# A third expert that runs on into the last ranking, one-hot products in place of a gather, and an order list made anew

## The chip, the cores and the metric

The kernel runs on one core of a Trainium2 chip. The metric is device microseconds of one execution, lower is better, given as the median of the runs shown. One more execution was taken with the hardware profiler, and all rows below are from it. Engines are named as in the profile: PE (TensorE matmul; PEld its weight loads), DVE (VectorE), ACT (ScalarE), POOL (GpSimd), SP (SyncE, which here issues DMAs only).

## The reference, cut to what matters

Two stages follow each other. The first is attention with a hash mask over 4 batches, 8 heads, 768 positions and 64 dimensions a head: a query sees a key only if all 6 sign bits of their projections agree. The second is a capacity expert: of each batch's 768 tokens the 128 with the highest gate score pass through a two-layer network and are added back.

```python
mask = q_bucket[:, :, :, None] == k_bucket[:, :, None, :]
scores = np.where(mask, scale * np.matmul(q, k.transpose(0, 1, 3, 2)), -1e9)
attn = np.exp(scores - np.max(scores, axis=-1, keepdims=True))
x = matmul(attn / (sum(attn) + 1e-9), v)      # then to (4, 768, 512)
scores = np.einsum('bsd,d->bs', x, w_gate)
for b in range(B):
    top_idx = np.argpartition(-scores[b], capacity)[:capacity]
    xe = x[b, top_idx]
    ye = np.maximum(xe @ w1, 0.0) @ w2
    out[b, top_idx] = xe + 1 / (1 + np.exp(-scores[b, top_idx]))[:, None] * ye
```

## The kernel before

There are 32 heads, numbered through all batches, so batch b is heads 8b to 8b+7. A head goes through these steps, each a small function that a word of a long list calls: load (X), split into two f16 parts (xh on ACT, xl on DVE), place by DMA (pa, pb, ps on SP's queue), row maxima in three pieces (mx and ma on PE, re on ACT, rd on DVE, line 550), scores in six units (s on PE, lines 584 and 587; e the exponential on ACT), a rest R = P minus its bf16 part in three pieces (two by r on DVE, line 617, one by g on POOL, line 620), the products with V in six chunks (a, line 642), the reciprocal (rc) and the normalised rows in the tile x (nw).

Three slots of two PSUM banks (`two`) and one of one bank (`one`) are shared by nearly all PE results; the string BANKS says which slot each use takes, and a use waits until the last reader of that slot is done.

The order in which each engine gets its instructions is written out by hand or by a planner in the string ORDER. A word is a function and its arguments, or the next step of a generator: c0 to c2 are `choose` (ranking of a batch), c3 `rank_last`, e0 to e2 `apply_expert`, e3 `apply_expert_last`. Every engine works its own instructions strictly in that order.

`turn` and `mine` deal with a resource that DVE and POOL share: an instruction of DVE with operands in SBUF is recorded by `mine`, and the next POOL subtraction (`turn`) waits for the last one recorded. Nothing makes the DVE instructions that come later wait for POOL.

For batches 0 to 2 `choose` makes the gate scores (line 694, tile `jks`, six instructions of 128x512, in two steps of three), turns them and sends them through DRAM, compares all pairs (lines 736 and 742), counts, makes a one-hot matrix `sel` (line 754), takes token numbers from it by products (line 803), and gathers the 128 chosen rows from `out` in DRAM by an indirect DMA. The expert then turns these rows (line 834), multiplies by w1 in three split products (line 870), takes the positive part, multiplies by w2 (line 892) and scatters the sum back (line 908).

For the last batch nothing follows that could cover this, so `rank_last` and `apply_expert_last` stand on the path to the end: scores, six f32 products that spread them over partitions (line 990), the comparisons, `sel`, the index product (line 1025), the index (line 1029), the gather, four transposes (line 834), the split (lines 842 to 846), and the two layers.

Of the kernel before, what the change touches and what calls it, by code (L numbers as in the profile page):

```python
# [52 lines left out]
ps.2.0 ma.1.0 rd.1.1 w vh.1 pb.1.2 rd.1.0 s.0.4 e.0.0 mt.1 vl.1 e.0.1 s.0.5 pb.1.3 mc2.1 mr.1 s.0.3 e.0.4 kv.2 X.7
pa.3.1 e.0.5 s.0.2 e.0.3 ps.3.0 mx.2.0 e.0.2 mx.2.2 sv.1 re.2.2 sh.1 r.0.0 re.2.0 a.0.0 r.0.2 mx.2.1 g.0.1 ma.2.2
sl.1 rd.2.2 a.0.1 ma.2.0 rd.2.0 re.2.1 xh.5 xh.7 s.1.3 ma.2.1 pa.4.0 s.1.0 s.1.2 rd.2.1 ps.3.1 pb.2.3 kv.3 pb.2.2
pb.3.2 e.1.3 pb.3.1 pb.3.3 e.1.0 X.8 pb.2.0 pb.2.1 xh.6 w a.0.2 xl.4 s.1.4 xl.5 xl.7 mt.2 mc2.2 mx.3.1 e.1.2 a.0.3
mr.2 pb.3.0 X.9 s.1.1 re.3.1 a.0.4 xl.6 mx.3.2 ma.3.1 e.1.1 a.0.5 rd.3.1 re.3.2 s.1.5 ma.3.2 h.1.0.4 e.1.4 rc.0
e.1.5 rd.3.2 pa.4.1 pb.4.0 g.1.1 nw.0 pa.5.0 sg.1.0.4 mx.3.0 r.1.0 re.3.0 s.2.0 ss.1.0.4 s.2.4 w s.2.1 ps.4.1
r.1.2 ma.3.0 e.2.0 e.2.4 s.2.2 a.1.0 s.2.3 e.2.1 e.2.2 a.1.1 rd.3.0 mt.3 w e.2.3 s.2.5 kv.4 mc2.3 ps.4.0 mx.4.0
pb.4.1 mx.4.2 pa.5.1 e.2.5 a.1.2 a.1.3 mr.3 g.2.1 re.4.0 mx.4.1 ma.4.0 r.2.0 ps.5.0 a.1.4 V.2 a.1.5 X.10 re.4.2  # L60
re.4.1 ma.4.2 s.3.5 w rd.4.0 ma.4.1 ps.5.1 xh.8 s.3.4 pb.4.2 w rd.4.2 pb.5.0 pa.6.0 rd.4.1 pa.6.1 pb.5.3 w e.3.5
e.3.4 s.3.0 mt.4 s.3.3 s.3.2 e.3.0 kv.5 mx.5.2 rc.1 nw.1 X.11 a.2.0 pb.4.3 mc2.4 e.3.3 mx.5.0 s.3.1 pb.5.2 re.5.2
# [124 lines left out]
def body(ctx, tc, qk, v, pj, wg, w1, w2, cst, cst16, out):  # L187
# [11 lines left out]
    def bank(name=None):  # L199
        return slots[int(next(banks))][:, 0]  # L200
# [521 lines left out]
    def put_out(b, half):  # L722
        d = slice(half * 256, half * 256 + 256)
        nc.scalar.dma_start(
            out[b].rearrange("(t p) d -> p t d", p=P)[:, :, d], st["x", b][:, :, d]
        )
# [369 lines left out]
```

## Time and profile before

| what | value |
|---|---|
| median of 3 runs | 421.06 us (420.73, 421.06, 422.6) |
| the profiled execution: its time | 423.3 us |
| its span, first to last instruction | 421.3 us |
| PE busy | 388.3 us, 92% of the span |
| DVE, ACT, POOL busy | 356.1, 287.2, 138.7 us |
| mean granted clock of TensorE | 0.969 of full |

The profiled execution lies 2.2 us above the median, and 2.0 us of it lie outside the span. Busy shares are means over the whole span, and this program has a long part in which PE hardly rests and a short part at its end in which it rests often, so they must be read by stretch.

### The profile page before, as it was taken

Reading aid. Unit: us, or ns where it says so; the run is one execution under the profiler, and the core shown is the slowest. Engines: PE = TensorE matmul, PEld = TensorE weight load, DVE = VectorE, ACT = ScalarE, POOL = GpSimd, SP = SyncE. Lnnn points to the kernel's source line nnn. Section 1 sums busy time; section 2 is a strip of 40 time slices with the busy share of each in tenths; the row PEclk is TensorE's granted clock in tenths of the full one; section 3 lists DMA queues with packets and bytes.
Section 4 is the critical chain, followed back from the end, with each engine's and each line's share of the span. In section 5 each row is a group of like instructions: output and inputs, shape, how many; then the busy total and the mean of one; then the engine's idle time right before and its main releaser. Section 6 shows DMA issues by size and latency. Waiting matters only on the chain.

```text
span 421.3 us, 13640 instructions
## 1 busy us (share of the span) xinstructions
PE 388.3 (92%) x5729; PEld 277.0 (66%) x5734; DVE 356.1 (85%) x585; ACT 287.2 (68%) x433; POOL 138.7 (33%) x91
## 2 busy tenths in 40 slices
PE   3799999999999999999799999999899999997385
PEld 1456776777667677786457777876557577875284
DVE  6879889899999999879979999769989898869521
ACT  4699988888889788866468787765667777441010
POOL 8115635243514284242432041250320434203000
PEclk9999999999999999999989999999989999999768
DMA  7746565383846542455445442325533331000500
GB/s 214 214 141 170 190 185 155 98 255 101 283 124 169 156 135 78 127 163 174 136 138 142 146 102 70 85 66 168 169 114 97 107 87 50 21 3 25 168 10 25
DMA packets 32940, 53.32 MB, mean 127 GB/s; under 512 B 5226, under 2 KB 24176, under 8 KB 32880
## 3 DMA queue, kind: packets, MB, share of 16 engines
q1 hardware_dynamic: 21696, 32.92, 27.9%
q10 hardware_dynamic: 10544, 17.43, 13.7%
q0 software_dynamic: 640, 2.10, 1.6%
q8 instruction: 45, 0.74, 0.8%
q14 instruction: 15, 0.12, 0.1%
HBM read 25.79 MB, written 7.35 MB: 79 GB/s over the span
## 4 chain that ended last, share of the span: by engine, by line
PE 70%; DVE 13%; issue 7%; DMA 5%; ACT 3%; SPq 1%; POOLq 0%; ACTq 0%; DVEq 0%
PE av L642 20%; PE two L584 11%; PE two L587 10%; PE two L524 6%; PE two L540 6%; PE one L870 3%; PE two L892 3%; PE one L584 3%; PE one L587 3%; DVE R L617 3%; DVE m L550 2%; PE two L331 2%; DMA A<-XH 2%; DVE jks L694 2%; DVE cm L736 1%
## 5 line engine op out<-in xcount | busy, mean ns | idle before, releaser
L620 POOL TENSOR_TENSOR R<-P 128x1536 f16<-128x1536 f32 x32 | 93.7, 2928 | 154.3 <-ACT P L600 25.3
L642 PEld LDWEIGHTS <-P 128*128 128x128 bf16 x2304 | 118.5, 97 | 17.4 <-issue 0.7
L642 PE MATMUL av<-V,P 128*128 128x65 f16 (+1 forms) x2304 | 123.6, 193 | 0.0
L642 PE MATMUL av<-V,R 128*128 128x65 f16 x1152 | 119.0, 192 | 0.0
L617 DVE TENSOR_TENSOR R<-P 128x1536 f16<-128x1536 f32 x64 | 114.8, 1804 | 2.7 <-ACT P L604 2.5
L604 ACT ACTIVATE P<-two 128x1024 f32<-128x1024 f32 x96 | 96.6, 1020 | 29.2 <-PE two L587 28.9
L550 DVE TENSOR_REDUCE m<-two 128x2 fp32r<-128x770 f32 x96 | 89.5, 952 | 20.4 <-PE two L540 20.1
L642 PEld LDWEIGHTS <-R 128*128 128x128 f16 x1152 | 105.5, 98 | 0.0
L584 PE MATMUL two<-A 97*128 97x512 f16 (+1 forms) x266 | 92.9, 357 | 5.9 <-DVE m L550 5.1
L587 PE MATMUL two<-B 128*128 128x512 f16 (+1 forms) x266 | 92.8, 356 | 0.0
L531 ACT ACTIVATE two<-two 128x770 f32<-128x770 f32 x96 | 75.0, 795 | 18.3 <-PE two L524 17.8
L587 PEld LDWEIGHTS <-B 128*128 128x128 f16 x384 | 38.1, 99 | 29.0 <-issue 7.8
L584 PEld LDWEIGHTS <-A 97*128 97x128 f16 x384 | 38.1, 99 | 25.9 <-issue 2.7
L524 PE MATMUL two<-kd,A 96*128 96x385 f16 x192 | 45.4, 330 | 3.5 <-DMA A<-sg 2.4
L540 PE MATMUL two<-A 96*128 96x385 f16 x192 | 46.4, 329 | 0.5 <-ACT two L531 0.5
L600 ACT ACTIVATE P<-one 128x512 f32<-128x512 f32 x59 | 35.0, 593 | 10.3 <-PE one L587 8.1
L416 DVE SCALAR_TENSOR_TENSOR XL<-X,XH 128x768 f16<-128x768 f32 x32 | 30.7, 978 | 0.5 <-DMA B<-XL 0.4
L600 ACT ACTIVATE P<-two 128x512 f32<-128x512 f32 x37 | 21.8, 592 | 12.6 <-PE two L587 10.9
L584 PE MATMUL one<-A 97*128 97x256 f16 x118 | 29.6, 275 | 0.0
L587 PE MATMUL one<-B 128*128 128x256 f16 x118 | 29.6, 275 | 0.0
L411 ACT ACTIVATE XH<-X 128x768 f16<-128x768 f32 x32 | 26.5, 836 | 0.9 <-DMA X<-in_qk_dram 0.7
L717 POOL TENSOR_TENSOR w1l<-W,w1h 128x512 bf16<-128x512 f32 x8 | 12.3, 1532 | 34.0 <-issue 12.3
(154 smaller groups left out, 502.5 us busy)
## 6 DMA issues: line engine op xcount, KB each, us to landing
X<-in_qk_dram SPq DMA_DIRECT2D x30, 384.0 KB
V<-in_v_dram ACTq DMA_DIRECT2D x16, 384.0 KB
B<-XL SPq DMA_DIRECT2D x64, 96.0 KB
B<-A SPq DMA_DIRECT2D x64, 96.0 KB
out_dram<-x ACTq DMA_DIRECT2D x8, 768.0 KB
A<-XH SPq DMA_DIRECT2D x62, 96.0 KB
W<-in_w_dram ACTq DMA_DIRECT2D x8, 512.0 KB
sbc<-scores SPq DMA_DIRECT2D x3, 384.0 KB
```

The costliest lines, as they stand in the source:

```text
L416: mine(nc.vector.scalar_tensor_tensor(xl, st["X", h], XS, st["XH", h], op0=ALU.mult, op1=ALU.subtract))
L524: nc.tensor.matmul(pt[:, i, : HS + 1], a[0:96, 0, q0 : q0 + P], kd, start=True, stop=False, skip_group_check=True,)
L531: nc.scalar.activation(o, o, AF.Relu)
L540: nc.tensor.matmul(pt[:, i, : HS + 1], a[0:96, 0, q0 : q0 + P], a[0:96, 1, HS : S + 1], start=False, stop=True, skip_group_check=True,)
L550: nc.vector.tensor_reduce(st["m", h][:, 2 * t : 2 * t + 2], st["mx", h, t][:, :, : HS + 1], axis=AX.X, op=ALU.max)
L584: nc.tensor.matmul(o, a[:, 1, k0 : k0 + P], a[:, 0, q0 : q0 + n], start=True, stop=False,)
L587: nc.tensor.matmul(o, bt[:, 1, k0 : k0 + P], bt[:, 0, q0 : q0 + n], start=False, stop=True,)
L600: nc.scalar.activation(pp[:, :, 512:S], pt.rearrange("p (a b) -> p a b", a=2), AF.Exp, scale=ES)
L604: nc.scalar.activation(pp[:, :, 0:512], pt, AF.Exp, scale=ES)
L617: mine(nc.vector.tensor_tensor(**rest(h, g)))
L620: turn(nc.gpsimd.tensor_tensor(**rest(h, g)))
L642: nc.tensor.matmul(o[:, t, 0:n], l, vv[:, c, hh, v0 : v0 + n], start=False, stop=last and l is lo, skip_group_check=True,)
```

## The change

Four things are changed. (1) The list ORDER and the string BANKS are replaced as a whole. The words are the same but for two more steps of c3; their places differ everywhere. (2) The tiles of `choose` (`sbc`, `sel`) get tags of their own, C1 and C3, no longer those of the expert (M1, M3); idx, xe and ss get three buffers, and the expert looks up its rows when it uses them. In the new list the last four of the 23 steps of e2 stand behind the last head's last product. (3) In the last batch the expert's input no longer comes through the gather and the transposes: `sel` is made in f32, and 24 f32 products of x with `sel` give the chosen rows already turned. A second `sel` in f16, the index and the gather follow behind; they are still needed for the gate and the sum at the end. The gate moves behind the first layer's products. (4) The second half of the last batch's `out` rows is sent from SP's queue, not from ACT's, and later.

```diff
-        sbc = sb.tile([P, NC, P], F32, tag="M1", name=f"sbc{b}", bufs=1)
+        sbc = sb.tile([P, NC, P], F32, tag="C1", name=f"sbc{b}", bufs=1)
...
-        sel = sb.tile([P, NC, P], F16, tag="M3", name=f"sel{b}", bufs=1)
+        sel = sb.tile([P, NC, P], F16, tag="C3", name=f"sel{b}", bufs=1)
...
     def apply_expert_last(b, tags):
 
         m = expert(b, tags)
-        m.turn_x(bank())
         m.split_x(both=True)
-        yield
-        m.gate()
         yield
         h = [bank(), bank()]
         m.up(h[0], 0, [(j, k, i) for i in range(3) for j in range(4) for k in range(4)])
         yield
         m.relu(h[0], 0)
         m.up(h[1], 1, [(j, k, i) for i in range(3) for j in range(4) for k in range(4)])
+        yield
+        m.gate()
         yield
         m.relu(h[1], 1)
         m.gate2()
...
     def rank_last(b):
...
         need(*(("nd", NH - 1, j) for j in range(3)))
-        put_out(b, 1)
...
+        put_out(b, 1, nc.sync)
         rp = bank()
...
-        sel = sb.tile([P, NC, P], F16, tag="XL", name=f"sel{b}", bufs=XLB)
+        sel = sb.tile([P, NC, P], F32, tag="P", name=f"sel{b}", bufs=PB)
+        select(rank, sel)
+        yield
+        xp = st["xp", b] = bank()
+        for k in range(4):
+            for t in range(NC):
+                nc.tensor.matmul(
+                    xp[:, k * P : (k + 1) * P], st["x", b][:, t, k * P : (k + 1) * P], sel[:, t],
+                    start=(k == 0 and t == 0), stop=(k == 3 and t == NC - 1), skip_group_check=True,
+                )
+        yield
+        sel = sb.tile([P, NC, P], F16, tag="XL", name=f"sel{b}_1", bufs=XLB)
+        select(rank, sel)
+        yield
         ip = bank()
-        select(rank, sel)
-        yield
...
-r.31.2 sc.3.1.5.6 a.31.4 a.31.5 e2 sc.3.1.3.4 rc.31 c3 nw.31 c3 c3 c3 c3 c3 c3 c3 c3 c3 c3 po.3.0 c3 c3 c3 c3 c3
-c3 c3 c3 c3 c3 c3 c3 c3 c3 c3 e3 e3 e3 c3 e3 e3 c3 e3
+sc.3.1.0.1 sc.3.1.1.2 rc.31 c3 e2 nw.31 e2 e2 c3 e2 c3 c3 c3 c3 c3 c3 c3 c3 c3 c3 c3 c3 c3 c3 c3 c3 c3 c3 c3 c3 c3
+c3 c3 c3 po.3.0 c3 e3 c3 e3 c3 e3 e3 e3 c3 e3
```

Three places show what the list moves. The first is PE's order where the last head's products with V (tile av, line 642) end and the spreading of the scores (tile sc) begins; before:

```order
L642 LDWEIGHTS P_2_7252
L642 MATMUL av_7418<-V_94,P_2_7252 128x64
L642 LDWEIGHTS R_2_7510
L642 MATMUL av_7418<-V_94,R_2_7510 128x65
L990 MATMUL one<-cs,sc_2_7560 128x128 x3
L990 MATMUL two_68<-cs,sc_2_7560 128x128 x3
```

and now, where hth and htl are the third expert's hidden values:

```order
L642 LDWEIGHTS R_2_7398
L642 MATMUL av_7400<-V_94,R_2_7398 128x65
L892 LDWEIGHTS hth_7299
L892 MATMUL one<-w2h,hth_7299 128x512
L892 LDWEIGHTS hth_7299
L892 MATMUL one<-w2l,hth_7299 128x512
L892 LDWEIGHTS htl_7300
L892 MATMUL one<-w2h,htl_7300 128x512
...
L988 MATMUL two_67<-cs,sc_2_7548 128x128 x3
L988 MATMUL two_69<-cs,sc_2_7548 128x128 x3
```

Twelve products of the third expert's second layer, four times these three, now stand between the two, where none stood.

The second place is PE's order between the last ranking and the last expert's first layer (tiles sel, xe the gathered rows, xth the split rows); before:

```order
L1025 LDWEIGHTS sel_7618
L1025 MATMUL one<-c_72,sel_7618 128x1
...
L834 MATMUL two_67<-cs,xe_7628 128x128 x4
L870 LDWEIGHTS w1h
L870 MATMUL one<-xth_7634,w1h 128x128
```

and now:

```order
L1025 MATMUL two_69<-sel_7617,x_6130 128x128 x24
L1035 LDWEIGHTS sel_1_7644
L1035 MATMUL one<-c_72,sel_1_7644 128x1
...
L870 LDWEIGHTS w1h
L870 MATMUL two_67<-xth_7646,w1h 128x128
```

The transposes of the gathered rows are gone from PE, 24 products with `sel` stand ahead of the index products, and the first layer follows without the gather.

The third place is DVE's order at the gate scores of the second batch (jks and sc are the scores, m the row maxima that free PSUM slots); before:

```order
L416 SCALAR_TENSOR_TENSOR XL_3996<-X_2595,XH_3371 128x768
L694 ISA jks_1_0_4035,sc_1_4034<-x_2360,wgt 128x512
...
L694 ISA jks_1_2_4039,sc_1_4034<-x_2360,wgt 128x512
L694 ISA sc_1_4034 128x1
L550 TENSOR_REDUCE m_4043<-two_69 128x2
L550 TENSOR_REDUCE m_4043<-two_68 128x2
L550 TENSOR_REDUCE m_4043<-two_67 128x2
```

and now, where all six scores stand together:

```order
L498 SCALAR_TENSOR_TENSOR W_82<-W_82,cs,two_68 128x2x65
L465 SCALAR_TENSOR_TENSOR V_94<-V_3739,V_94 128x12x64
L904 SCALAR_TENSOR_TENSOR ye_4045<-one,ss_3293,xe_3158 128x512
L694 ISA jks_1_0_4058,sc_1_4057<-x_2373,wgt 128x512
...
L694 ISA jks_1_5_4068,sc_1_4057<-x_2373,wgt 128x512
L694 ISA sc_1_4057 128x1
L550 TENSOR_REDUCE m_4089<-two_69 128x2
L617 TENSOR_TENSOR R_2_4136<-P_2_3995 128x1536
```

One row maximum, not three, waits behind the scores here. In ORDER the POOL subtraction nearest ahead of these scores (g.16.1) stood directly before them; now it follows r.16.0 and stands ten DVE instructions ahead of them. At the third batch's scores the nearest one (g.24.1) stood before them and now stands behind them.

## Rows read from the trace of the kernel before

**Rows 1.** Busy time by stretch (us, engines, granted clock, DMA share, GB/s).
```profile
207.50:210.50 3.00, 0.16 (x2) 0.09 (x1) 3.00 (x6) 0.60 (x1) 0.81 (x1) 1.00 0.71 250
210.50:214.00 3.50, 3.50 (x10) 1.23 (x10) 3.50 (x8) 1.10 (x2) 0.00 (x0) 0.51 0.79 277
214.00:303.50 89.50, 89.36 (x1401) 64.93 (x1402) 78.73 (x128) 66.72 (x100) 25.78 (x10) 1.00 0.40 109
303.50:306.00 2.50, 0.27 (x2) 0.10 (x1) 2.50 (x8) 0.40 (x1) 0.00 (x0) 1.00 1.07 374
306.00:309.50 3.50, 3.50 (x13) 1.60 (x11) 3.50 (x5) 1.51 (x2) 0.00 (x0) 0.52 0.60 200
391.00:395.00 4.00, 1.71 (x19) 1.04 (x19) 4.00 (x17) 0.48 (x1) 0.00 (x0) 0.98 1.06 372
395.00:401.00 6.00, 0.82 (x9) 0.49 (x9) 1.70 (x5) 0.00 (x0) 0.97 (x1) 0.50 0.18 48
401.00:408.50 7.50, 6.91 (x58) 6.48 (x59) 1.73 (x4) 0.84 (x3) 0.00 (x0) 0.50 0.00 0
```
**Rows 2.** Waits of PE: line, waited for, us in total, times, longest.
```profile
PE two L584 <- DVE m L550: 5.1, 2, 2.8
```
**Rows 3.** Timeline of DVE, POOL and PE at 205 us: start, duration, instruction, idle before.
```profile
204.57 0.68 DVE L694 CUSTOM_DVE_ANT_0 jks<-x,wgt 128x512 bf16<-128x512 f32 x1
205.18 3.69 DVE L694 CUSTOM_DVE_ANT_0 jks<-x,wgt 128x512 bf16<-128x512 f32 x1
209.41 2.68 DVE L550 TENSOR_REDUCE m<-two 128x2 fp32r<-128x770 f32 x3
205.54 2.77 POOL L620 TENSOR_TENSOR R<-P 128x1536 f16<-128x1536 f32 x1
210.41 0.49 PE L584 MATMUL two<-A 97*128 97x512 f16 x1 [2.84 <-DVE m L550]
```
**Rows 4.** The same at 300 us.
```profile
300.44 3.23 DVE L694 CUSTOM_DVE_ANT_0 jks<-x,wgt 128x512 bf16<-128x512 f32 x1
300.12 3.00 POOL L620 TENSOR_TENSOR R<-P 128x1536 f16<-128x1536 f32 x1 [1.37 <-ACT P L604]
305.82 0.38 PE L584 MATMUL two<-A 97*128 97x512 f16 x1 [2.23 <-DVE m L550]
```
**Rows 5.** Timeline of PE: first and last of three second-layer products.
```profile
200.02 0.38 PE L892 MATMUL two<-w2h,hth 128*128 128x512 f16 x1
...
200.45 0.38 PE L892 MATMUL two<-w2h,htl 128*128 128x512 f16 x1
```
**Rows 6.** Timeline of the last ranking and expert, all engines, in order of time.
```profile
386.02 0.75 DVE L904 SCALAR_TENSOR_TENSOR ye<-two,ss,xe 128x512 f32<-128x512 f32 x1
387.29 0.17 DVE L652 TENSOR_SCALAR rc<-av 128x6 f32<-128x6 f32 x1 [0.19 <-PE av L642]
389.36 0.93 PE L990 MATMUL one<-cs,sc 128*128 128x128 f32 x6 [2.10 <-DVE sc L981]
390.13 0.83 PE L990 MATMUL two<-cs,sc 128*128 128x128 f32 x6
390.89 0.48 DVE L736 TENSOR_SCALAR_CACHE_REDUCE cm<-sbc,sc 128x256 bf16<-128x256 f32 x1 [1.13 <-ACT sbc L995]
395.90 0.96 DVE L754 TENSOR_TENSOR sel<-c,rank 128x768 f16<-128x768 f16 x1
397.27 0.16 DVE L1029 TENSOR_SCALAR idx<-one 128x1 int32<-128x1 f32 x1 [0.41 <-PE one L1025]
401.04 1.12 PE L834 MATMUL two<-cs,xe 128*128 128x128 f32 x4 [3.81 <-DMA xe<-out_dram,idx]
402.62 2.11 PE L870 MATMUL one<-xth,w1h 128*128 128x128 f16 x16 [0.47 <-ACT xth L842]
410.01 1.06 PE L870 MATMUL two<-xtl,w1h 128*128 128x128 f16 x16
410.90 0.27 PE L892 MATMUL one<-w2h,hth 128*128 128x256 f16 x1
```

More of the change, by code (lines that the diff above doesn't have):

```diff
@@ L53 @@
[L53 to L62, printed above, removed]
@@ L720, in load_w, with put_out @@
             yield
-    def put_out(b, half):
+    def put_out(b, half, eng=None):
         d = slice(half * 256, half * 256 + 256)
-        nc.scalar.dma_start(
+        (eng or nc.scalar).dma_start(
             out[b].rearrange("(t p) d -> p t d", p=P)[:, :, d], st["x", b][:, :, d]
@@ L805, in choose @@
         yield
-        idx = sb.tile([P, 1], I32, tag="idx", name=f"idx{b}", bufs=2)
+        idx = sb.tile([P, 1], I32, tag="idx", name=f"idx{b}", bufs=3)
         nc.vector.tensor_scalar(idx, ip[:, 0:1], float(b * S), None, op0=ALU.add)
-        gather(b, idx, sb.tile([P, DM], F32, tag="xe", name=f"xe{b}", bufs=2))
+        gather(b, idx, sb.tile([P, DM], F32, tag="xe", name=f"xe{b}", bufs=3))
     def gather(b, idx, xe):
@@ L832, in turn_x @@
             t["xp"] = xp
+            xe = st["xe", b]
             for k in range(4):
@@ L838, in split_x @@
         def split_x(both=False):
-            xp = t["xp"]
+            xp = t["xp"] if "xp" in t else st["xp", b]
             xh, xl = tile_("xth", 512, F16), tile_("xtl", 512, F16)
@@ L849, in gate @@
         def gate():
-            ss = sb.tile([P, 2], F32, tag="ss", name=f"ss{b}", bufs=2)
+            ss = sb.tile([P, 2], F32, tag="ss", name=f"ss{b}", bufs=3)
             jk = tile_("ye", DM, F32)
             mine(nc.vector.tensor_tensor_reduce(
-                out=jk, in0=xe, in1=wgt, op0=ALU.mult, op1=ALU.add,
+                out=jk, in0=st["xe", b], in1=wgt, op0=ALU.mult, op1=ALU.add,
                 scale=1.0, scalar=0.0, accum_out=ss[:, 0:1],
@@ L904, in finish @@
             nc.vector.scalar_tensor_tensor(
-                ye, yp[:, : f.stop - f.start], t["ss"][:, 1:2], xe[:, f], op0=ALU.mult, op1=ALU.add
+                ye, yp[:, : f.stop - f.start], t["ss"][:, 1:2], st["xe", b][:, f], op0=ALU.mult, op1=ALU.add
             )
@@ L908, in finish @@
                 nc.gpsimd.indirect_dma_start(
-                    out=out2, out_offset=bass.IndirectOffsetOnAxis(ap=idx[:, 0:1], axis=0), in_=t["ye"],
+                    out=out2, out_offset=bass.IndirectOffsetOnAxis(ap=st["idx", b][:, 0:1], axis=0), in_=t["ye"],
                     in_offset=None,
@@ L1019, in rank_last @@
         nc.vector.tensor_tensor(rank, rp[:, :NC], acc, op=ALU.add)
-        sel = sb.tile([P, NC, P], F16, tag="XL", name=f"sel{b}", bufs=XLB)
-        ip = bank()
+        sel = sb.tile([P, NC, P], F32, tag="P", name=f"sel{b}", bufs=PB)
         select(rank, sel)
         yield
+        xp = st["xp", b] = bank()
[9 more added lines that the diff above has]
+        yield
+        ip = bank()
         for t in range(NC):
@@ L1027, in rank_last @@
             )
-        idx = sb.tile([P, 1], I32, tag="idx", name=f"idx{b}", bufs=2)
+        idx = sb.tile([P, 1], I32, tag="idx", name=f"idx{b}", bufs=3)
         nc.vector.tensor_scalar(idx, ip[:, 0:1], float(b * S), None, op0=ALU.add)
```

213 lines of the change are left out of this document (111 added, 102 removed), and 8 rows, old and new, of the table BANKS.

## The prediction

> **What bounds the kernel now.** I read the busy time by stretch first. Over the long part PE is the bound: it worked 89.36 of 89.5 us in the stretch from 214, at full clock [rows 1]. So work taken off PE there shortens the program, and idle time of PE there lengthens it. Two stretches break the pattern: PE did almost nothing in 207.5 to 210.5 and 303.5 to 306.0, and its granted clock was then 0.51 and 0.52 for 3.5 us each [rows 1]. The list of PE's waits names the cause as far as PE sees it: score products waiting for a row maximum on DVE, twice, 5.1 us [rows 2]. Third, the timeline around both. At 205 us DVE's gate score, 0.68 us elsewhere, lasted 3.69 us, almost exactly until POOL's subtraction (205.54, 2.77 us) was over; the three row maxima stood behind it, all three two-bank slots stayed full, and PE waited 2.84 us [rows 3]. At 300 us the same happened: a score of 3.23 us beside a POOL subtraction of 3.00 us, and PE waited 2.23 us [rows 4]. Last, the tail from 387 us on: there nothing is covered, and every step of the last ranking and expert counts [rows 6].
>
> **What the first wait cost.** 2.84 us idle, and 3.5 us at 1.2 GHz instead of 2.4, in which PE did half the work: 1.75 us. Together 4.6 us; the second one 2.23 + 1.75 = 4.0 us [rows 1, 3, 4]. Sum 8.6 us.
>
> **The rule behind it.** The trace shows the hold: 3.69 against 0.68 us beside one POOL instruction [rows 3]. The Trainium skill (SBUF — State Buffer, Who interferes with whom) says that the two engines share a port pair by an exclusive lock: whichever issues first keeps it, the other is blocked for the whole instruction. By that rule DVE's score, recorded as starting at 205.18, should have won over POOL's 205.54; the rows show it losing, so the recorded start doesn't tell who wins, and I give a POOL subtraction near a score an even chance of costing DVE its full length.
>
> **The change, term by term.** All sums are differences in the profiled execution (423.3 us, of which 2.0 lie outside the span); I apply them to the median, 421.06 us.
>
> (a) Twelve products of the third expert move from before the end of the last head to behind it. PE is the bound there, a product takes 0.215 us (three of them start at 200.02 to 200.45, two steps) [rows 5]: 12 x 0.215 = -2.58 us. The other 19 steps of this expert stay in front, so "during the ranking" is true of this little only.
>
> (b) Behind it they cost less. The score chain on DVE takes from about 387.1, when the last product with V ended and the wait of 0.19 us began, to 389.36, so the spreading products began 2.3 us after it [rows 6]; now PE is free 2.58 us after it, plus a little: +0.33 us. The sum of the third expert on DVE (0.75 us) falls into the 1.13 us in which DVE waited for the spread scores [rows 6]; without that cover it would cost those 0.75. The scatter and the last two halves of `out` now leave some 4 us later than before, on POOL, SP and ACT; the queue of SP holds nothing else then, and the gather that must wait for them is issued some 20 us after the last head, so they cost nothing.
>
> (c) In the last selection, from the end of `sel` (396.86) to the end of the transposes (402.16), 5.3 us go: index products, index, gather and transposes [rows 6]. In their place come 24 f32 products. The nearest rows are the six spreading products, also f32, 128x128, one weight load each: six records are three products, and six products took from 389.36 to 390.96, 0.267 us each, at full clock [rows 6]. So 24 take 6.4 us at 2.4 GHz and 12.8 us at 1.2 GHz. Which clock? PE has nothing but counting products for some 5.9 us before them, as before; the granted clock fell within that stretch before (0.98 in 391 to 395, 0.50 after), and within 3 us of the idle starts at 207.5 and 303.5 [rows 1]. So they start at 1.2 GHz. It came back after some 3.5 us of steady work in the two stalls, and only at 408.5 in the tail, 5.9 us after the first layer began at 402.62 [rows 1, 6]. I take the middle, 4.7 us: in these half speed loses 2.35 us, 6.4 + 2.35 = 8.75 us. The first layer then runs at full clock where it ran mostly at half: sixteen products take 0.89 us (410.01 to 410.90) [rows 6], 96 take 5.35; with 0.77 us for the split ahead of it, the second layer begins 8.75 + 0.77 + 5.35 = 14.9 us after `sel`, before it was 410.90 - 396.86 = 14.0. Term: +0.85 us. Bounds: full clock throughout 6.4 + 0.77 + 5.35 = 12.5, so -1.5; half clock throughout the products and the first layer as before, 14.0 - 5.3 + 12.8 = 21.5, so +7.5.
>
> The tail's 5.9 us hold four transposes ahead of the first layer [rows 6]. The Trainium skill (TensorE: Matmul & The Clock Gate, Part 4: PE-mode transpose) says that transposes don't count as work for the clock. Products with `sel` are no transposes; by that rule the two stalls would be the better model, the products would take 6.4 + 1.75 = 8.2 us and the term would be +0.3. No run here shows it for f32 products.
>
> The gather is now covered: the index can be ready some 1.8 us after the products (behind the split on DVE), the rows 3.7 us later (397.27 to 401.0 before) [rows 6], the gate about 1 us after that, by the like gate score of 0.68 us and an exponential [rows 3]. This meets the end of the first layer at 6.1 us within a few tenths, and 24 second-layer products of 0.11 us (half the columns of those of 0.215) that need only the first half of it (2.6 us) lie behind. If the gather took 2.5 us longer, it would begin to cost.
>
> (d) The list. `sel` in f32 on DVE has as many elements as in f16 (0.96 us) [rows 6]; I take no difference; twice the time would be +1.0. The tags of their own let `choose` start beside an expert, which matters only through the list. What the list is worth I read from the two stalls: in the new one no POOL subtraction stands directly ahead of the second and third batch's scores, and behind the second's six scores stands one row maximum, not three. So both stalls in their present form should go: up to -8.6 us. Against this stands that every POOL subtraction, one a head, can hold DVE up, in a list whose new neighbours no row shows, and that six scores in one piece keep DVE away from PSUM for some 4 us. Bounds: -8.6 and 0, and below nothing a third stall, +4.3. I take the middle of the first two, one stall of this size left somewhere: -4.3 us.
>
> Sum: -2.58 + 0.33 + 0.85 - 4.3 = -5.7 us, so 415.4 us.
>
> **Rivals.**
> - The list gains nothing: the two stalls turn up at other places. For it: the list before was made for the same work and got two in three batches. Against: the scores, the only places where a hold reached PE, are now clear. -2.58 + 0.33 + 0.85 = -1.4: 419.7 us.
> - Both stalls go and none comes: -10.0: 411.1 us. For it the order at the scores; against, that holds of DVE come by chance of arrival.
> - Slower, by the list: one stall more than before, as when all three batches' scores meet a POOL subtraction or six scores in one piece fill the slots: -1.4 + 4.3 = +2.9: 424.0 us. It decides from about 1.4 us of new idle time of PE on, with nothing recovered.
> - Slower, by the clock: the f32 products never bring the clock back, and the first layer starts at 1.2 GHz too. For it: counting products didn't hold the clock [rows 1]; against: after the six f32 products at 389 to 391 us the clock was still 0.98 over the next 4 us [rows 1], so they may count. -2.58 + 0.33 + 7.5 = +5.3 with no gain of the list: 426.3; with half of it 422.0. Alone it decides when the products take over 10.2 us, which is a clock back later than 7.6 us after their start.
>
> **How the numbers follow.** Forecast 0.36, list without gain 0.22, both stalls gone 0.15, list with another stall 0.17, clock 0.10. About 2.1 us, 0.5%, is what a measurement of this kernel can tell from no change. Faster by more: the forecast, both stalls gone and the lower part of the second case, 0.57; within: most of "without gain" and half of the clock case, 0.21; slower: 0.22. The range 410.5 to 424 leaves out the clock case with no gain and the tails of its neighbours; the likeliest case's own range, from -1.5 to +2 of term (c) and a stall more or less in size, is 413 to 417.5.
>
> **What would show it.** Right: PE busy without a break and clock 1.00 around the second and third batch's scores; the last product with V some 2.6 us plus the recovered stalls earlier; 24 products that start at 1.2 GHz and end at 2.4, 8 to 9.5 us long; a second layer that doesn't wait for the gate. Wrong: scores of 3 us again; products of 12 us; DVE's second half of the hidden values waiting for the gather; or a last product with V as late as before.

## The result, and the profile after

The changed kernel took 426.28 us (median of 4 runs, 426.0 to 426.7) beside 420.89 us for the kernel before on the same chip: a ratio of 1.0121, with a 95% interval of 1.0092 to 1.015. Timed again later (e15 below) it was 1.0111, interval 1.0088 to 1.0135. It is slower by 5.4 us; I had forecast 415.4 us, 5.7 us faster, and the range ended at 424. (Ratios leave disturbed runs out and medians don't, so the two can differ by some tenths of a per cent.)

The profiled execution (426.7 us, span 424.9) is split here at the same places of the program as the one before: the first product with V of heads 0, 16 and 20. The columns are those of [rows 1]; a stretch's length less its PE time is what TensorE stood idle. The first two stretches of the kernel before, and its last one, from head 28 to the last product with V:

```profile
30.03:204.38 174.35, 173.00 (x2679) 123.33 (x2673) 160.56 (x239) 144.24 (x221) 72.80 (x33) 1.00 0.55 158
204.38:252.62 48.24, 45.36 (x675) 31.04 (x673) 44.74 (x79) 35.93 (x53) 16.00 (x6) 0.96 0.49 142
...
352.58:387.25 34.67, 34.56 (x629) 27.25 (x628) 28.17 (x53) 14.82 (x22) 8.47 (x4) 1.00 0.07 20
```

The same two of the changed kernel, the last heads from 28 on, and three short stretches that the text comes to:

```profile
30.10:213.84 183.74, 175.86 (x2693) 124.55 (x2693) 163.82 (x245) 145.82 (x223) 68.19 (x36) 1.00 0.54 154
213.84:260.11 46.27, 44.51 (x679) 30.94 (x678) 42.08 (x78) 36.24 (x55) 13.83 (x6) 1.00 0.50 141
...
357.46:390.14 32.68, 32.63 (x622) 26.38 (x622) 27.74 (x54) 16.22 (x26) 8.24 (x3) 1.00 0.03 9
345.59:347.66 2.07, 0.00 (x1) 0.03 (x1) 0.29 (x1) 0.00 (x0) 1.58 (x1) 1.00 0.52 188
347.77:351.18 3.41, 3.41 (x35) 2.66 (x35) 1.77 (x3) 2.22 (x3) 0.00 (x0) 0.50 0.02 5
399.00:405.80 6.80, 5.75 (x27) 5.78 (x28) 1.77 (x2) 0.00 (x0) 0.00 (x0) 0.50 0.43 152
```

Heads 0 to 16 took 174.35 us and take 183.74; TensorE's idle time in them rose from 1.35 to 7.88 us, and the rest of the difference, 2.9 us, is work that the new list does earlier. Heads 16 to 20, with the first of the two old stalls, went from 48.24 to 46.27 us. The stalls of [rows 3, 4] are gone: all six scores of a batch run in one piece at 0.68 or 0.69 us. Shown are the first and last score of the second batch and of the third, then POOL beside the second batch's scores, where it has a scatter and no subtraction:

```profile
212.63 0.68 DVE L694 CUSTOM_DVE_ANT_0 jks<-x,wgt 128x512 bf16<-128x512 f32 x1
...
215.69 0.68 DVE L694 CUSTOM_DVE_ANT_0 jks<-x,wgt 128x512 bf16<-128x512 f32 x1
...
304.64 0.68 DVE L694 CUSTOM_DVE_ANT_0 jks<-x,wgt 128x512 bf16<-128x512 f32 x1
...
307.70 0.69 DVE L694 CUSTOM_DVE_ANT_0 jks<-x,wgt 128x512 bf16<-128x512 f32 x1
```
```profile
205.91 2.75 POOL L620 TENSOR_TENSOR R<-P 128x1536 f16<-128x1536 f32 x1 [4.84 <-DVE R L617]
...
213.00 1.19 POOL L908 DMA_INDIRECT out_dram<-ye,idx  x1 [2.66 <-DVE ye L904]
```

What came in their place is TensorE's list of waits in the changed kernel (columns of [rows 2]). From head 0 to the last product with V the kernel before had its two stalls, 5.1 us, and three more waits of 1.0, 0.8 and 0.3 us; now there are fifteen, of 0.2 to 2.1 us:

```profile
...
PE one L834 <- DMA xe<-out_dram,idx: 3.0, 3, 2.1
PE two L540 <- ACT two L531: 2.1, 2, 1.2
PE two L584 <- ACT P L604: 1.9, 3, 1.2
PE one L584 <- DMA A<-mr: 1.7, 1, 1.7
PE two L584 <- ACT P L600: 1.4, 1, 1.4
...
PE two L584 <- DMA A<-mr: 1.3, 1, 1.3
...
PE two L584 <- DVE m L550: 1.1, 2, 0.5
...
```

They have no common cause: gathers (L834), a row of maxima that SP moves into A (A<-mr), exponentials on ACT (P), a ReLU on ACT (L531), row maxima on VectorE (m). The largest is the wait for the third expert's gather (timeline of the changed kernel, POOL and PE):

```profile
342.15 2.24 POOL L812 DMA_INDIRECT xe<-out_dram,idx  x1 [11.89 <-DVE idx L807]
...
347.66 1.00 PE L834 MATMUL one<-cs,xe 128*128 128x128 f32 x4 [2.07 <-DMA xe<-out_dram,idx]
```

TensorE had nothing for 2.07 us and then ran 3.41 us at 0.50 of its clock (the rows at 345.59 and 347.77 above): the same effect as in the two stalls that went, at a new place and by another cause.

The tail, in answer to [rows 6] (timeline of the changed kernel, all engines):

```profile
390.18 0.17 DVE L652 TENSOR_SCALAR rc<-av 128x6 f32<-128x6 f32 x1 [1.77 <-PE av L642]
...
392.56 1.50 PE L988 MATMUL two<-cs,sc 128*128 128x128 f32 x12
392.77 0.75 DVE L904 SCALAR_TENSOR_TENSOR ye<-one,ss,xe 128x512 f32<-128x512 f32 x1
...
393.94 0.48 DVE L736 TENSOR_SCALAR_CACHE_REDUCE cm<-sbc,sc 128x256 bf16<-128x256 f32 x1 [0.43 <-ACT sbc L993]
...
398.95 1.83 DVE L754 TENSOR_TENSOR sel<-c,rank 128x768 f32<-128x768 f16 x2
400.05 8.34 PE L1025 MATMUL two<-sel,x 128*128 128x128 f32 x48 [1.34 <-DVE sel L754]
408.23 0.29 PE L1035 MATMUL one<-c,sel 128*128 128x1 f16 x6
...
408.86 0.27 PE L870 MATMUL two<-xth,w1h 128*128 128x128 f16 x2 [0.34 <-ACT xth L842]
...
410.33 0.97 POOL L812 DMA_INDIRECT xe<-out_dram,idx  x1 [15.54 <-DVE idx L1039]
...
414.57 0.27 PE L892 MATMUL two<-w2h,hth 128*128 128x256 f16 x1
414.60 0.69 DVE L852 CUSTOM_DVE_ANT_0 ye<-xe,wgt 128x512 f32<-128x512 f32 x1 [1.13 <-DMA xe<-out_dram,idx]
```

The spreading products start 2.4 us after the last product with V instead of 2.1; the 24 f32 products (48 records) fill 400.05 to 408.23, at half clock until 405.8; the second layer begins at 414.57 without waiting for the gate.

**Where the 3.6 us of the span went.** Up to the last product with V: 387.25 us before, 390.14 after, +2.89. Idle time of TensorE from the start to there, summed over all gaps: 17.85 and 24.64, +6.79 (1.1 of it ahead of head 0's first product with V). Its busy time: 369.40 and 365.50, -3.90. Of these, 1.71 are the clock's: 10.24 us at 1.2 GHz before, 6.83 after, one stretch of 3.41 fewer. The other 2.2 are the work of the twelve products, which (a) priced at 2.58. Behind the last product with V: 34.02 before, 34.79 after, +0.77. The time of the runs rose by 5.4 us and that of the profiled executions by 3.4 (423.3 to 426.7), so about 2 us of the difference lie in the spread of the runs and can't be placed by one trace.

### The profile page after: what moved, and what is told of

Same layout as the page of the kernel before. It is cut to its first block, busy times and chain, and to the rows that moved or that the text cites. A ratio compares the mean times of both kernels' runs of the same rounds, so it can differ in the third digit from the quotient of the medians.

```text
span 424.9 us, 13706 instructions
## 1 busy us (share of the span) xinstructions
PE 391.0 (92%) x5771; PEld 281.3 (66%) x5778; DVE 350.9 (83%) x586; ACT 287.3 (68%) x433; POOL 130.2 (31%) x91
## 4 chain that ended last, share of the span: by engine, by line
PE 58%; DMA 15%; DVE 12%; issue 7%; ACT 5%; POOL 1%; SPq 1%; ACTq 0%; POOLq 0%; DVEq 0%
PE av L642 15%; PE two L584 8%; PE two L587 8%; DMA xe<-out_dram,idx 5%; PE two L540 5%; PE two L524 4%; DVE R L617 3%; PE one L892 3%; PE one L870 3%; DVE m L550 3%; DMA A<-XH 2%; DMA A<-mr 2%; DMA B<-XL 2%; PE two L1025 2%; DMA out_dram<-x 2%
## 5 line engine op out<-in xcount | busy, mean ns | idle before, releaser
L620 POOL TENSOR_TENSOR R<-P 128x1536 f16<-128x1536 f32 x32 | 87.9, 2748 | 162.9 <-DVE R L617 36.4
L617 DVE TENSOR_TENSOR R<-P 128x1536 f16<-128x1536 f32 x64 | 112.0, 1764 | 3.0 <-ACT P L604 2.0
L584 PE MATMUL two<-A 97*128 97x512 f16 (+1 forms) x290 | 96.9, 344 | 5.8 <-ACT P L604 1.9
L587 PE MATMUL two<-B 128*128 128x512 f16 (+1 forms) x290 | 96.7, 343 | 0.0
L531 ACT ACTIVATE two<-two 128x770 f32<-128x770 f32 x96 | 75.1, 798 | 15.1 <-PE two L524 13.0
L600 ACT ACTIVATE P<-two 128x512 f32<-128x512 f32 x49 | 28.8, 592 | 15.1 <-PE two L587 15.1
L600 ACT ACTIVATE P<-one 128x512 f32<-128x512 f32 x47 | 27.8, 590 | 3.4 <-PE one L587 2.6
L584 PE MATMUL one<-A 97*128 97x256 f16 x94 | 23.3, 273 | 1.7 <-DMA A<-mr 1.7
L540 PEld LDWEIGHTS <-A 96*128 96x128 f16 x192 | 16.1, 98 | 11.3 <-issue 3.9
L587 PE MATMUL one<-B 128*128 128x256 f16 x94 | 23.3, 273 | 0.0
```

Source lines behind the costliest of these rows:

```text
L531: nc.scalar.activation(o, o, AF.Relu)
L540: nc.tensor.matmul(pt[:, i, : HS + 1], a[0:96, 0, q0 : q0 + P], a[0:96, 1, HS : S + 1], start=False, stop=True, skip_group_check=True,)
L584: nc.tensor.matmul(o, a[:, 1, k0 : k0 + P], a[:, 0, q0 : q0 + n], start=True, stop=False,)
L587: nc.tensor.matmul(o, bt[:, 1, k0 : k0 + P], bt[:, 0, q0 : q0 + n], start=False, stop=True,)
L600: nc.scalar.activation(pp[:, :, 512:S], pt.rearrange("p (a b) -> p a b", a=2), AF.Exp, scale=ES)
L617: mine(nc.vector.tensor_tensor(**rest(h, g)))
```

## The experiments

Theory: the remade list costs the time, in small waits all over it, and the tail is nearly free. Rival: the f32 products or the products moved behind the last head cost it. All ratios are to the kernel before, timed beside each kernel on the same chip. Line numbers in these kernels are 2 lower than in the changed kernel (e15 is that kernel itself). The slot string BANKS changes together with ORDER in all of them but e4 and e15, and no run separates the two: how much of the waits for a PSUM slot comes from the slots and not from the order stays open.

**e1 and e2: each half alone.** e1 has the new list up to the last head and the old tail, e2 the old list and the new tail.

```diff
 e1: ORDER up to rc.31: new        rank_last, apply_expert_last: before's
 e2: ORDER up to rc.31: before's   rank_last, apply_expert_last: new
```


> The changed kernel's order list, slots and buffers up to the last head, with the kernel before's tail behind it: index, gather of the last tokens from memory, transposes. Theory 'the list is to blame' (the new list loses about 5.5 us up to the last head; the f32 one-hot products behind it cost nearly nothing): 425 to 427, within 1.5 us of the changed kernel, with the last av about 390 us after the span's start as there. Rival 'the f32 products are to blame': 420 to 422.

> The changed kernel's code and its tail (f32 one-hot products, expert without gather), behind the kernel before's list up to the last head, with e2's second layer where it was before. Theory 'the list': 420.5 to 422.5, that is the kernel before plus 0.4 to 1.2 us, last av near 387 us. Rival 'the f32 products cost the 5 us': about 426.

e1: 429.02 us, 1.0143 (1.0084 to 1.0202). e2: 423.91 us, the median of all twelve runs, 1.6 us above that of the kernel before beside it (422.3); the ratio is 1.000 (0.9959 to 1.004). In e2's profile (425.78 us) the tail took 34.5 us, 0.5 more than before. The list is to blame; the tail adds about 1.6 us at most. But e1 is above what I expected: its last product with V ended at 389.3 us, near the changed kernel's 390.1, while its tail took 39.1 us instead of 34. e3 shows why.

**e3: only the 12 products moved.** 

```diff
-a.31.0 sc.3.1.2.3 e2 sc.3.1.1.2 g.31.1 e2 a.31.1 e.31.4 e2 sc.3.1.0.1 a.31.2 a.31.3
-r.31.2 sc.3.1.5.6 a.31.4 a.31.5 e2 sc.3.1.3.4 rc.31 c3 nw.31 c3 c3
+a.31.0 sc.3.1.2.3 sc.3.1.1.2 g.31.1 a.31.1 e.31.4 sc.3.1.0.1 a.31.2 a.31.3
+r.31.2 sc.3.1.5.6 a.31.4 a.31.5 sc.3.1.3.4 rc.31 c3 e2 nw.31 e2 e2 c3 e2 e2 c3
```


> The kernel before with one thing changed: the last four second-layer steps of e2 (12 products) and its finish stand behind the last head's normalisation, among the last ranking's steps. My terms (a) and (b): 12 x 0.215 us leave the full stretch, 0.33 us comes back behind: -2.25 us, so 418.3 to 419.3. Rival 'the ranking behind the last head is full as well, the products only move': within 0.5 us of before (420.4 to 421.4).

425.49 us, 1.0079 (1.0045 to 1.0113): slower, which neither side had. POOL, ACT's queue and PE in e3, in order of time:

```profile
396.21 1.06 POOL L906 DMA_INDIRECT out_dram<-ye,idx  x1 [10.81 <-DVE cm L740]
399.03 0.40 ACTq L722 DMA_DIRECT2D out_dram<-x  x1
403.37 0.96 POOL L810 DMA_INDIRECT xe<-out_dram,idx  x1 [6.10 <-DMA out_dram<-x]
...
406.70 1.11 PE L832 MATMUL two<-cs,xe 128*128 128x128 f32 x4 [7.71 <-DMA xe<-out_dram,idx]
```

The scatter of the third batch, the last store of `out` and the last batch's gather all touch the same tensor in memory and go one behind the other: the store was issued when the scatter was down, and the gather 4.3 us later, when the store was. Before, the scatter left at 387.05 and the gather waited for its index only. With the products behind the last head, the scatter leaves some 9 us later and the gather with it. And up to the last head little was won: from head 28 to the last product with V e3 took 34.4 us instead of 34.7, because TensorE waited 2.0 us there (e7 names for what).

**e12: e3 with that chain cut.** The third expert's finish, with its scatter, stands behind the last gather.

```diff
-c3 e2 e2 c3 c3
+c3 e2 c3 c3
...
-c3 c3 e3 e3
+c3 c3 e2 e3 e3
```


> e3 (the kernel before, e2's last 12 products behind the last head, the last tokens still gathered from the output in memory) with e2's finish, its sum and its scatter to the output, put behind the last batch's gather. Theory 'in e3 the gather stood behind the scatter and the second store of the last batch, which all write or read the same output': the 6.1 us of waiting on POOL goes, the tail is 34 to 34.5 us instead of 38.6, and the time 420.5 to 422.5 (0.996 to 1.001 of the kernel before; e3 was 1.008). Rival 'the products behind the last head cost the time themselves': 425, as e3.

423.27 us, 1.0045 (1.0009 to 1.008). In the profile the tail is 34.6 us, as expected, and POOL and PE read:

```profile
399.30 0.97 POOL L810 DMA_INDIRECT xe<-out_dram,idx  x1 [13.91 <-DVE idx L1027]
402.70 0.71 PEld L832 LDWEIGHTS two<-cs,xe 128*128 128x128 f32 x4 [3.96 <-DMA xe<-out_dram,idx]
```

The gather waits for its index again. The chain is shown for the tail; the total missed the expected 0.996 to 1.001, because the stretch up to the last head is no shorter than before (388.25 us, idle 21.5 where it was 17.9; 2.0 of that is the wait that e3 has).

**e4: the two stalls alone.** In the kernel before, POOL's weightings of heads 16 and 24 (the subtractions of [rows 3, 4]) are put behind the first or second ranking step of the next batch.

```diff
-re.18.0 g.16.1 re.18.2 po.1.0 pb.19.2 s.17.1 c1 ma.18.0
+re.18.0 re.18.2 po.1.0 pb.19.2 s.17.1 c1 g.16.1 ma.18.0
...
-pb.27.2 g.24.1 mx.26.1 ma.26.0 e.24.5 a.24.1 ma.26.2 s.25.1 re.26.1 ma.26.1 pb.27.1 c2 pb.27.3 c2 rd.26.0
+pb.27.2 mx.26.1 ma.26.0 e.24.5 a.24.1 ma.26.2 s.25.1 re.26.1 ma.26.1 pb.27.1 c2 pb.27.3 c2 g.24.1 rd.26.0
```


> The kernel before with two words of its list moved: POOL's weighting of heads 16 and 24 (the product g that holds VectorE's port) starts after the first ranking step of the next batch's choice instead of before it, so that the gate score no longer stands in VectorE's queue beside it. My pricing of the two stalls (2.84 and 2.23 us without work on TensorE, and 1.75 us each for the stretch at 1.2 GHz behind them): 412 to 414 if both go, 416 to 418 if one goes. Rival 'a stall gives back slack that other work takes, or the wait moves to another place': 420 to 422. That would mean that my term for the list was wrong already in its size, not only in what the new list does.

415.35 us, 0.9832 (0.9773 to 0.9891): 7 us. Heads 16 to 20 took 44.2 us instead of 48.24, heads 24 to 28 48.2 instead of 52.2: 4.1 and 4.0 us, 8.0 in all, where I had priced 4.6 and 4.0. DVE and POOL in e4 at the first place:

```profile
207.20 0.69 DVE L692 CUSTOM_DVE_ANT_0 jks<-x,wgt 128x512 bf16<-128x512 f32 x1
207.82 2.69 DVE L548 TENSOR_REDUCE m<-two 128x2 fp32r<-128x770 f32 x3
...
210.94 0.68 DVE L692 CUSTOM_DVE_ANT_0 jks<-x,wgt 128x512 bf16<-128x512 f32 x1
```
```profile
208.06 2.74 POOL L618 TENSOR_TENSOR R<-P 128x1536 f16<-128x1536 f32 x1 [1.12 <-DVE sc L692]
```

The two stretches in e4, heads 16 to 20 and 24 to 28:

```profile
205.80:249.97 44.17, 43.75 (x675) 30.58 (x673) 41.88 (x79) 35.54 (x53) 16.02 (x6) 1.00 0.55 157
298.02:346.23 48.21, 47.23 (x699) 32.82 (x697) 45.00 (x81) 36.91 (x57) 16.79 (x6) 1.00 0.41 113
```

The subtraction now lies beside three row maxima, which take 0.9 us each as elsewhere, and holds nobody. So the size of the stalls was read rightly to within 0.6 us; the changed kernel did get rid of them, and its new waits cost more than they had.

**e5: one wait of the new list mended.** The third expert's transposes and split stand later, so the gather has time to land.

```diff
-a.27.0 e2 re.30.1 ma.30.1 rd.30.0 rd.30.1 mx.30.2 a.27.1 e2 g.27.1 e.28.4 r.27.2 a.27.2 s.28.5
-a.27.3 re.30.2 pb.30.0 r.28.0 s.29.2 ma.30.2 a.27.4 e.28.5
+a.27.0 re.30.1 ma.30.1 rd.30.0 rd.30.1 mx.30.2 a.27.1 g.27.1 e.28.4 r.27.2 a.27.2 s.28.5
+a.27.3 e2 re.30.2 pb.30.0 r.28.0 s.29.2 ma.30.2 a.27.4 e2 e.28.5
```


> The changed kernel with two words of its list moved: e2's transposes stand four steps of TensorE later (behind a.27.3) and the split of them behind a.27.4, so that the gather has about 3.3 us more to land. In the changed kernel TensorE waited 2.07 us for it at 345.6 us and ran 3.4 us at 1.2 GHz behind it. Theory 'the new list loses its time in such waits, each at full price': 2.07 us and 1.7 us come back, about 422.5 beside 426.3 for the changed kernel (ratio to the kernel before 1.003 to 1.006). Rival 'one wait removed only moves the same slack to the next engine': 425.5 to 426.5 (1.012).

422.84 us, 1.0005 (0.9974 to 1.0037). The wait at 345 us and the low stretch behind it are gone (340 to 352 us: PE busy 11.79 of 12.00, clock 1.00). Two words of the list brought back some 4.5 us by the ratios, 3.8 expected. The profile is of the slowest of e5's twelve runs (425.81 us), so only this stretch is read from it; at 152.45 us it has another wait of 2.00 us, for an exponential, with a low stretch of its own.

**e9: the old list up to head 16, then the new one.**

```diff
-ORDER = new list
+ORDER = before's list up to a.16.5, then the words of the new list that are left, in its order
```


> The changed kernel's code; its list follows the kernel before's up to the last av of head 16 and the new list from there (two PSUM slots renumbered at the seam). Up to head 16 the new list had 7.6 us more without work on TensorE (19.13 against 11.51), in a dozen waits of 0.3 to 1.7 us; from there to the last head it had 5.5 against the old list's 6.3. Theory 'the loss of the new list sits in the small waits of its first half': 418 to 419.5 (0.991 to 0.996 of the kernel before), idle time up to head 16 about 12 us. Rival 'the loss is spread, or is given back behind the seam': 422 to 426.

427.63 us, 1.0127 (1.0071 to 1.0182): a miss. Head 16 was reached at 206.6 us with 12.4 us idle, 7.3 us earlier than in the changed kernel, but behind the seam it all went (busy time by stretch, heads 0 to 16 and 16 to 20):

```profile
31.50:206.56 175.06, 173.39 (x2680) 123.34 (x2673) 160.51 (x239) 144.22 (x221) 72.79 (x33) 1.00 0.56 156
206.56:264.16 57.60, 51.08 (x692) 33.88 (x690) 47.40 (x84) 38.74 (x58) 17.40 (x7) 0.91 0.43 127
```

57.60 us for what takes 46 to 48: the seam kept the old stall (2.84 us for a row maximum) and put three more waits (0.8 to 1.6 us) and 10.2 us at half clock behind it. It tells nothing on the first half, so it was made again.

**e13, e14, e15: the seam behind the stalls.** e13 takes e4's list up to head 20 and the new list from there; e14 adds e5's edit; e15 is the changed kernel.

```diff
-ORDER = new list
+ORDER = e4's list up to a.20.5, then the words of the new list that are left, in its order   (e13)
+       the same, with e2's transposes and split moved as in e5                               (e14)
```


> The changed kernel's code; its list follows the old list (with POOL's weightings of heads 16 and 24 moved, as in e4) up to the last av of head 20, and the new list from there. Theory 'first half': up to head 20 the new list stood 20.9 us without work on TensorE, the moved old list 13.2 to 14.3, so 6.6 to 7.7 us come back: 418.5 to 420 (0.990 to 0.996 of the kernel before). Rival 'the loss is spread over the list': 423 to 426, as the changed kernel.

> e13 with e5's edit: e2's transposes and their split later in the list. If the waits add up, 3.8 us below e13: 415 to 416 (0.982 to 0.987 of the kernel before). Rival 'the second edit finds its slack already used': equal to e13.

> The changed kernel, unchanged, beside e13, e14 and e16: 1.009 to 1.015 of the kernel before, as when it was first timed. It is the anchor for the differences between them; no theory hangs on it.

e15 426.35 us, 1.0111 (1.0088 to 1.0135); e13 419.19 us, 0.9931 (0.9902 to 0.996); e14 416.53 us, 0.9895 (0.9865 to 0.9925). Busy time of e13 from head 0 to 20:

```profile
29.76:249.41 219.65, 217.28 (x3352) 153.81 (x3346) 202.69 (x317) 179.88 (x273) 88.82 (x38) 1.00 0.55 156
```

and of e15:

```profile
30.19:259.74 229.55, 220.24 (x3373) 155.53 (x3371) 206.01 (x323) 182.16 (x277) 82.22 (x41) 1.00 0.54 151
```

Idle 2.4 us against 9.3: 6.9 us, and e13 is 7.2 us faster than e15. So the small waits of the new list's first 20 heads cost their time; they aren't slack. That the two numbers lie so close is partly chance: the stretch is 9.9 us shorter in e13, since the new list also does 3 us of work earlier, and behind the seam heads 20 to 28 took 100.1 us in e13 and 96.8 in e15. e14's edit brought 2.7 us more by the medians and 1.5 by the ratios, whose intervals overlap, where 3.8 were expected; in e13 that wait was 1.8 us and had no low stretch behind it.

**e6 and e7: the two new parts on a list without the stalls.** e6 is e4 with the new tail, e7 also has the 12 products behind the last head.

```diff
 e6: ORDER of e4 up to rc.31, then the new tail without e2
 e7: the same; the last five e2 behind rc.31, as in e3
```


> The kernel before's list with POOL's weighting of heads 16 and 24 moved (experiment e4) and behind the last head the changed kernel's tail: f32 one-hot products in place of index, gather and transposes on the path; e2 stays in front. By my term (c) the tail costs +0.85 us; by the old-list run with the new tail +0.4: 0.984 to 0.986 of the kernel before. Rival 'the f32 products cost more where e2's products do not stand ahead of them': 0.988 or more.

> As e6, and the last 12 second-layer products of e2 with its finish behind the last head, as in the changed kernel. In e3 this move made the kernel slower, because the last batch's gather, which reads the output in memory, started only when e2's scatter and both stores of the last batch had landed (6.1 us of waiting on POOL, 7.7 us on TensorE). Theory 'that chain is the price, and the one-hot products take it off the path': faster than e6 by what e3 gained up to the last av, 0.5 to 2.3 us (1.6 us of the 2.58 us went there into a wait for POOL's R of the last head): 0.979 to 0.984 of the kernel before. Rival 'the move itself costs, by its place in the ranking': slower than e6 by 3 us, 0.991.

e6: 413.78 us, 0.9821 (0.9761 to 0.9881); e7: 415.86 us, 0.9857 (0.9799 to 0.9915); the runs can't tell the two apart. e7's tail is 33.5 us, so with the gather off the path the chain of e3 is harmless. But the products gave nothing up to the last head: 379.1 us in e6, 379.6 in e7. TensorE's waits in e7 from 345 us on:

```profile
PE av L640 <- POOL R L618: 1.6, 1, 1.6
PE av L640 <- DVE R L615: 0.4, 1, 0.4
```

The products that left had covered the last head's residuals R on POOL and DVE.

**e8 and e10: the clock of the f32 products.** Thirteen idle products fill TensorE's gaps in the last ranking, in the changed kernel (e8) and in e6 (e10).

```diff
-    def warm_last():
+    def warm_last(n):
         wp = bank()
-        for i in range(WARM):
+        for i in range(n):
             nc.tensor.matmul(wp, w1h[:, 0, 0:P], w1h[:, 0, 0:512], start=True, stop=True)
...
+c3 wl.3 c3 c3 wl.1 c3 c3 wl.2 c3 c3 wl.1 c3
...
+c3 wl.6 c3 po.3.0
```


> The changed kernel with 13 idle products (512 columns of f16 each, into a slot of PSUM that nobody reads) put into TensorE's gaps during the last ranking: 3, 1, 2 and 1 behind the ranking's first steps, 6 while VectorE builds the f32 one-hot table. They compute nothing that is used. Theory 'the clock is lost to the idle time in the ranking, and half of the f32 products then run at 1.2 GHz': the 48 product records take 5.3 to 6 us in place of 8.2, and the kernel ends 1.5 to 2.9 us earlier (423.4 to 424.8 beside 426.3). Rival 'idle products delay the ranking, or the clock falls all the same': 426 to 428.

> e6 (the old list with POOL's two weightings moved, f32 one-hot products behind the last head) with the 13 idle products of e8 in the gaps of the last ranking. They compute nothing that is used. By e8's tail (33.4 us against 34.8 for the changed kernel): 1 to 2 us below e6, 0.977 to 0.980 of the kernel before; the low stretch of the clock, 10.2 us in e6, shortens to 3.4 to 7. Rival 'the gain of e8 was another kernel's': equal to e6, 0.982.

e8: 424.08 us, 1.0049 (1.0012 to 1.0085); e10: 413.61 us, 0.980 (0.9747 to 0.9854). TensorE in e8:

```profile
399.19 6.26 PE L1023 MATMUL two<-sel,x 128*128 128x128 f32 x48
```

The products took 6.26 us, of which 1.5 at half clock (low stretch 397.3 to 400.7). In e10 no part of them is at half clock, and the next product follows 5.43 us after the first of them, 0.23 us for each of the 24:

```profile
389.60 5.60 PE L1023 MATMUL two<-sel,x 128*128 128x128 f32 x48
395.03 0.29 PE L1033 MATMUL one<-c,sel 128*128 128x1 f16 x6
```

The tail was 33.4 us in e8, where two executions of the changed kernel have 34.8 and 33.8 (e15), and between e6 and e10 it went from 33.8 to 32.5. The gain in the traces is thus 0.4 to 1.4 us; in e8 the idle products also delay the ranking, so that the f32 products start 10.7 us after the last product with V instead of 9.9. Between e6 and e10 the runs can't tell the gain (0.982 and 0.980).

**e11 and e16: all together.** e11 is e10 up to head 28 and the new list from there; e16 is e14 with the idle products.

```diff
 e11: ORDER of e4 up to a.28.5, then the rest of the new list, wl words in the tail
 e16: ORDER of e14, wl words in the tail
```


> As e10, but from the last av of head 28 on the new list takes over, with e2's last products behind the last head and the new list's order of POOL's and VectorE's residuals R of the last heads (the e2 steps that the old list has done by then are not repeated). In e7 the 2.58 us taken out of the last heads came back as waits for R (1.6 us POOL, 0.4 us VectorE); the changed kernel has no such wait there. Theory 'the move of the 12 products pays where R is early enough': 1.5 to 2.3 us below e10, 0.972 to 0.976 of the kernel before. Rival 'the last heads are bound by VectorE and POOL in any order': equal to e10 within 0.5 us.

> e14 with the idle products of e8 and e10 in the gaps of the last ranking (they compute nothing that is used): 1 to 2 us below e14, 413 to 415, and within 1 % of e11 (0.974), whose second half is mostly the old list. If the new list's second half holds the 12 products behind the last head without a wait, as it did in the changed kernel, e16 equals e11 within 2 us; rival 'the small waits of the new list's second half still cost': 3 us or more above e11.

e11: 410.88 us, 0.9743 (0.969 to 0.9797), the fastest of all, 11 us below the kernel before beside it (422.15). Against e10 the intervals overlap, and the two profiled spans are equal (411.9 and 411.7), so the runs leave open what the 12 products bring there. The traces have a part of it: from head 28 to the last product with V e11 (first row) took 1.9 us less than e10, and its tail took 0.9 us more (33.4 and 32.5).

```profile
345.69:378.48 32.79, 32.19 (x619) 25.99 (x618) 26.50 (x52) 14.97 (x22) 8.24 (x3) 1.00 0.06 19
344.60:379.26 34.66, 34.66 (x630) 27.26 (x628) 28.19 (x53) 14.83 (x22) 8.49 (x4) 1.00 0.07 20
```

e16: 415.49 us, 0.9854 (0.9828 to 0.9881), 4.6 us above e11: its rival held. The new list's heads 20 to 28 have waits of their own (1.2 and 0.7 us for P, 1.0 for a ReLU in the trace).

## Why the prediction was wrong

**The step that failed is (d), the list.** "Up to -8.6 us" for the two stalls was nearly right (e4: 8.0 us in their stretches, 7 in the runs). "I take the middle of the first two, one stall of this size left somewhere: -4.3 us", with a bound of +4.3, was wrong in kind. I priced a wholly new list by the two places where the old one showed a hold, and took all its other handovers to be as good as before. Measured up to the last product with V: 6.79 us more idle and 1.71 us won by the clock, +5.1 us where -4.3 was forecast. With the 8.6 us that did go, the new waits cost 13.7. None of the rivals had this either: "one stall more" is a single mechanism of 4.3 us, while the new list lost by fifteen waits of 0.2 to 2.1 us, on ACT, VectorE and two kinds of DMA, one of them with a low clock. The old list's 1.35 us idle in 174 us of heads 0 to 16 said how tight it was: there was hardly anything to win outside the stalls, and much to lose.

The lists themselves could have given a warning. Between the last step of the third batch's choice (its gather) and the first step of its expert (transposes of what it gathers) the old list has fifteen steps of scores and products with V, the new one three: s.28.3, s.28.4 and a.27.0. Between the move of a head's maxima into A (`mr`) and that head's first score product, the old list has 39 such steps in all for heads 1 to 15, the new one 21; two of the new waits, 1.7 and 1.3 us, are for exactly that move. These counts were made with the waits in hand, and they don't fit everywhere: between the second batch's gather and its expert the old list has 2 such steps and no wait, the new one 7 and a wait of 0.4 us, and for heads 16 to 31 the second count is 29 in the old list and 36 in the new.

**Rival "slower, by the list".** The sign was its sign and the place its place; its price, one stall, was a third of the waits found.

**(a) -2.58 us** was a little too much: the work that left is 2.2 us, and from head 28 to the last product with V the changed kernel took 32.68 us instead of 34.67, both with at most 0.1 us idle. (Behind that product stand five steps of this expert, four of three products each and its finish, not the four that I counted; 18 stay in front.) It is no property of the move: in e7 and e3 2.0 us of it turned into waits for R.

**(b) +0.33 us, the rest for nothing.** The start of the spreading products moved by 0.3 us, and VectorE's sum (0.75 us) lies ahead of a remaining wait of 0.43 us. "The scatter and the last two halves cost nothing" was right only because the last tokens no longer come by a gather; with the gather on the path the same move cost 4.6 us (e3). I had not seen that the two parts of the change need each other.

**(c) +0.85 us.** (b) and (c) together were +1.18; measured +0.77. That they lie so close is in part luck. A product is 0.22 to 0.23 us at full clock, not 0.267; and the clock came back 5.7 us after the products began, not 4.7, so that they took 8.2 us, forecast 8.75. But this time isn't fixed. In e15, the same kernel, it was 3.8 us and the products took 7.2:

```profile
399.15 7.38 PE L1025 MATMUL two<-sel,x 128*128 128x128 f32 x48 [1.34 <-DVE sel L754]
```

In e2, e5, e6, e7, e9, e13 and e14 it was 3.0 to 5.5 us. The old tail varies as well: 34.0 us in the kernel before, 32.7 in e4, where its low stretch was 10.2 us and not 13.7. The tail's +0.77 is within this spread. The Trainium skill (TensorE: Matmul & The Clock Gate, Part 4: PE-mode transpose) says that transposes don't count as work for the clock. The prediction took from it the model of the two stalls, the clock back after 3.5 us and products of 8.2 us. The total of 8.2 us agrees by chance: the clock was back after 5.7 us then, and where it was back after 3.8 us the products took 7.2. No run here tests the rule on transposes itself. That f32 products do count as work the run shows: the clock rose at 405.8 us while only they ran (400.05 to 408.23). `sel` in f32 took 0.96 us, as in f16.

**The hold of VectorE** (3.69 us beside a subtraction) was read rightly, e4 shows it. The Trainium skill (SBUF — State Buffer, Who interferes with whom) also says that on trn2 a `tensor_reduce`, as the row maxima are, never contends with POOL. e4's rows agree: a subtraction of 2.74 us beside three maxima of 0.9 us each, neither held.

## What to carry to other kernels

A new order of a full engine is a change of every handover in it, not of the two places where the old order was seen to fail. Before giving the list any credit, look for each handover at how many steps of the bound engine lie between producer and consumer, in the old list and in the new; a drop is a place to doubt, though the count alone didn't tell all waits here. In a list with 1% idle time, mend the stalls by moving single words; two words here brought 7 us, a remade list lost 5. Before work is moved behind a store, a scatter and a gather of one tensor, follow that chain: what costs nothing with the gather off the path costs its whole length with it on.

## What the runs showed of the hardware

With idle products in its gaps TensorE lost the clock all the same, for a shorter time: in e8 it was recorded busy 4.24 of the 5 us from 391 to 396 (before 391 to 395: 1.71 of 4 [rows 1]), and the clock fell at 397.3, just behind the counting products; it was back after 3.4 us instead of 6.8. A gather beside other transfers took 5.5 us from its issue to the products that need it (342.15 to 347.66), in the quiet tail 3.4 (399.30 to 402.70 in e12). A low clock doesn't follow every wait: in the changed kernel the waits of 1.7, 1.3 and 1.4 us between 39 and 110 us left it at 1.00, the one of 2.07 us was followed by 3.41 us at 0.50. Nor does the length of the wait alone decide: in e15 the clock stayed at 1.00 after a wait of 2.23 us at 39.6 us and fell to 0.50 for 3.41 us after one of 1.88 us at 344.9, and in e13 it stayed after 1.78 us at 339.5.
